# Transposing the maxima directly behind the value sums, and reading the memory in 64 by 64 quarters

## The chip, the cores and the metric

The kernel runs on one core of one Trainium2 chip. The metric is the device time of one launch in microseconds. In a profile the engines are called PE (TensorE's matmuls), PEld (its weight loads), DVE (VectorE), ACT (ScalarE), POOL (GpSimd) and SP (SyncE, which issues most transfers); ACTq and SPq are the queues of ScalarE and SyncE where they issue a transfer.

## The reference

Four attention layers, A B A B, each with a layer norm ahead and a residual add behind, over a sequence of 2048 tokens, width 512, 32 heads of 16. A is linear attention with a learned feature map. B, which the change touches, is causal-style softmax attention in four segments of 512 tokens with a compressive memory (the mask adds -1e9 to every later-indexed key):

```python
for s in range(N):                                   # N = 4 segments
    qs, ks, vs = q[:, :, s], k[:, :, s], v[:, :, s]
    logits = jnp.einsum("bhqd,bhkd->bhqk", qs, ks) * scale + mask
    p = _softmax(logits, axis=-1)
    a_dot = jnp.einsum("bhqk,bhkd->bhqd", p, vs)
    pq = phi(qs)
    num = jnp.einsum("bhld,bhde->bhle", pq, M)
    den = jnp.einsum("bhld,bhd->bhl", pq, z)[..., None] + 1e-6
    a_mem = num / den
    o = g * a_mem + (1.0 - g) * a_dot
    outs.append(o)
    pk = phi(ks)
    M = M + jnp.einsum("bhld,bhle->bhde", pk, vs)
    z = z + jnp.einsum("bhld->bhd", pk)
```

## The kernel before, in words

All engines' instruction orders are written out by hand: every instruction is tied to the one before it on its engine, so each engine works strictly in the order in which the program emits. Layer B is emitted by `steps`, a loop over slots. The work is cut into 32 half-blocks `m` per layer (4 segments, 4 groups of eight heads, 2 halves of four heads), and each half-block has five slots; slot `m.j` of a segment is its slot j of half-block m (0 to 7).

Each slot first emits one step of `attend` (logits into the PSUM tile `lg`, which has one buffer; then one exponential of 128 x 1024 on ScalarE into a `P` tile, and a triangular select on GpSimd) and one step of `maxima` (query-key products of a half-block two ahead, whose row maxima VectorE takes from PSUM with `mask` added; results in `mxs`). Then come functions put aside in the slot before (`self.later`), and jobs filed under the slot's number (`self.at`: copies and casts of projections, on ScalarE, VectorE and GpSimd). In a slot m.0 `weighted` follows: the value sums of the half-block just finished, 16 matmuls with 32 columns of the array each, into one `g` tile, which ScalarE copies, scaled by `share`, into `U`. After that the slot's own words from the tables FIRST (segment 0), GAPS (segments 1 and 2), LAST and FINAL (segment 3 of the first and the second layer B) are carried out from left to right:

- `max` is `put_maxima`: the 128 x 16 maxima are transposed on TensorE into a `g` tile, ScalarE copies them negated into `mt`, and ScalarE's own queue issues the transfer of `mt` into row 63 of the query stack `Q` that `attend` of the next half-block uses.
- `fin` is `finish`: four transposes of `U` into a `g` tile, then `weigh` on VectorE: a reciprocal and a multiplication, which read the `g` tile.
- `a0` to `a3` are `reads` of the memory for head groups 0 to 3 of this segment (`a0+`: of the next): `phi` of the queries (`tb` tiles) times `kn` (`mem`). Each word does one half: a `g` tile, two plain fp32 matmuls of the whole array, 136 wide, then `weigh` with three instructions on VectorE. `kn` holds zeros outside its own heads: rows 0 to 63 serve heads 0 to 3 of the group, rows 64 to 127 heads 4 to 7.
- `t`, `m` are the two steps of `writes` (four transposes of key features; then 16 small matmuls and the update of the memory on VectorE and GpSimd); `turn` is four transposes of finished outputs with a copy on ScalarE and a subtraction on VectorE (`oh`, `ol`); `ln` is a step of the next norm, in these places `columns`: four transposes with a copy and a subtraction (`hh`, `hl`).
- In slots m.1 to m.4 stand the large products in quarters: `Q` (query and key projection, two at once), `V` (values, two at once), `O` and `P` (output projections, two at once). Each such pair takes two `g` tiles when it begins and runs half the rows of the array for one and half for the other, in turns.

The PSUM tag `g` has four buffers of one bank each (`G = 4`); a tile takes the one that came free first, and its first matmul waits until the previous owner's last reader is done. Slots m.2 and m.4 use two `g` tiles for the maxima (`SPARE`), m.0, m.1 and m.3 the tiles `mx` and `my`. Helpers record every operation, so in the profile L178 is every matmul, L182 every transpose, and L156 nearly everything else.

Of the kernel before, what the change touches and what calls it, by code (L numbers as in the profile page):

```python
# [7 lines left out]
F32 = mybir.dt.float32  # L8
F32R = mybir.dt.float32r
BF16 = mybir.dt.bfloat16  # L10
AF = mybir.ActivationFunctionType
# [7 lines left out]
P = 128  # L19
# [3 lines left out]
VW = DH + 1  # L23
# [7 lines left out]
MT = 2  # L31
G = 4
# [20 lines left out]


FIRST = """
0.0 max            | 0.2 Q2/6          | 0.3 Q2/12         | 0.4 Q2/6
1.0 t0 fin max     | 1.1 Q3/6          | 1.2 Q3/6          | 1.3 Q3/6 | 1.4 Q3/6
2.0 m0 ln ln ln ln max fin | 2.1 V+/6     | 2.2 V+/6 w        | 2.3 V+/6 | 2.4 V+/6 w
3.0 t1 fin max     | 3.1 V+/6          | 3.2 V+/6 w        | 3.3 V+/6 | 3.4 V+/6 w
4.0 m1 max fin     | 4.1 Q0+/6 load    | 4.2 Q0+/6         | 4.3 Q0+/6 | 4.4 Q0+/6  # L60
5.0 t2 fin max     | 5.1 V+/6          | 5.2 V+/6 n        | 5.3 V+/6 n | 5.4 V+/6
6.0 m2 t3 fin max  | 6.1 Q1+/6         | 6.2 Q1+/6 n       | 6.3 Q1+/6 n | 6.4 Q1+/6
7.0 m3 a0+ a0+ max fin | 7.1 V+/6      | 7.2 V+/6 n        | 7.3 V+/6 n | 7.4 V+/6
"""
GAPS = """
0.0 a1 a1 max fin  | 0.1 Q2/6 n        | 0.2 Q2/6 n        | 0.3 Q2/6 n | 0.4 Q2/6
1.0 t0 turn fin max | 1.1 Q3/6      | 1.2 Q3/6 n        | 1.3 Q3/6 | 1.4 Q3/6
2.0 m0 turn t1 fin ln max | 2.1 O/6    | 2.2 O/6           | 2.3 O/6 | 2.4 O/6
3.0 m1 turn turn fin ln max | 3.1 O/6  | 3.2 O/6           | 3.3 O/6 | 3.4 O/6
4.0 ln ln a2 fin a2 max | 4.1 Q0+/6 load | 4.2 Q0+/6       | 4.3 Q0+/6 | 4.4 Q0+/6  # L70
5.0 t2 a3 fin max  | 5.1 V+/6 begin  | 5.2 V+/6 n N      | 5.3 V+/6 n N | 5.4 V+/6
6.0 m2 a3 t3 fin max | 6.1 Q1+/6       | 6.2 Q1+/6 n N     | 6.3 Q1+/6 n N | 6.4 Q1+/6
7.0 m3 a0+ a0+ max fin | 7.1 V+/6      | 7.2 V+/6 n N      | 7.3 V+/6 n N | 7.4 V+/6
"""
LAST = """
0.0 a1 a1 max fin  | 0.1 Q2/6 n        | 0.2 Q2/6 n        | 0.3 Q2/6 n | 0.4 Q2/6
1.0 turn max fin   | 1.1 Q3/6          | 1.2 Q3/6 n        | 1.3 Q3/6 | 1.4 Q3/6
2.0 turn ln fin max | 2.1 O/6          | 2.2 O/6           | 2.3 O/6 | 2.4 O/6
3.0 turn turn fin ln max | 3.1 O/6     | 3.2 O/6           | 3.3 O/6 | 3.4 O/6
4.0 ln ln a2 fin a2 max | 4.1 v/2      | 4.2 v/2           | 4.3 v/2 | 4.4 v/2  # L80
5.0 a3 a3 max fin  | 5.1 v/1           | 5.2 v/1           | 5.3 v/1 | 5.4 v/1
6.0 max fin        | 6.1 v/1           | 6.2 v/1           | 6.3 v/1 | 6.4 v/1 pre
7.0 pt pt fin max  | 7.1 P/4           | 7.2 P/5           | 7.3 P/5 v/2 | 7.4 P/4 v/2
"""
FINAL = """
0.0 a1 a1 max fin  | 0.1 Q2/6          | 0.2 Q2/6          | 0.3 Q2/6 | 0.4 Q2/6
1.0 turn turn max fin | 1.1 Q3/6       | 1.2 Q3/6          | 1.3 Q3/6 | 1.4 Q3/6
2.0 max fin        | 2.1 O/6           | 2.2 O/6           | 2.3 O/6 | 2.4 O/6
3.0 a2 a2 max fin  | 3.1 O/6           | 3.2 O/6           | 3.3 O/6 | 3.4 O/6
4.0 turn turn fin max | 4.1 O/6        | 4.2 O/6           | 4.3 O/6 | 4.4 O/6  # L90
5.0 a3 a3 max fin  | 5.1 O/6           | 5.2 O/6           | 5.3 O/6 | 5.4 O/6
6.0 max fin pre    | 6.1 pt pt         | 6.2 P/6           | 6.3 P/6 | 6.4 P/6
7.0 pt pt max fin  | 7.1 P/4           | 7.2 P/5           | 7.3 P/5 | 7.4 P/4
"""
BEFORE = {-25: "q0 load", -23: "v0", -21: "k0",
          -18: "n", -17: "v1 n", -16: "n", -15: "n n", -14: "q1 n", -13: "n", -12: "k1 n", -11: "n", -10: "v2 n",
# [4 lines left out]
def interleave_kernel(ctx, tc, x_in, a_wqkv, a_wphi, a_wo, b_wq, b_wk, b_wv, b_wo, b_beta,  # L101
# [15 lines left out]
    def nm(s):  # L117
        uid[0] += 1
        return f"{s}_{uid[0]}"

    def T2(tag, bufs, dt=F32, shape=(P, 512)):
        return sp.tile(list(shape), dt, tag=tag, bufs=bufs, name=nm(tag))

    def PS(tag, bufs, shape=(P, 512)):
        return ps.tile(list(shape), F32, tag=tag, bufs=bufs, name=nm(tag))
# [38 lines left out]
    dve, act, pool, sync = [Ordered(e) for e in (nc.vector, nc.scalar, nc.gpsimd, nc.sync)]  # L164

    def held(i):

        if last[0] is not None:
            behind(i, last[0])
        last[0] = i  # L170
        return i
# [3 lines left out]
    def mm(*a, **k):  # L175
        n = a[0].free_size()
        work[0] += n / 2.26 if k["rhs"].dtype == F32R else (n * 2 / 2.4 + 25 if "tile_position" in k else 2 * max(112, n * 2 / 2.4))
        return held(nc.tensor.matmul(*a, **k))  # L178

    def tp(*a):  # L180
        work[0] += 108
        return held(nc.tensor.transpose(*a))  # L182
# [338 lines left out]
    def weigh(out, p, eps, add, eng=pool):  # L521

        n, G = out.shape[1], out.shape[2]
        r = T2("r", 4, shape=(P, n, G))
        den = p[:, :, :, DH]
        if eps:
            dve.tensor_scalar(r, den, eps, None, op0=ADD)
            den = r
        dve.reciprocal(r, den)
        rb = r.unsqueeze(3).broadcast_to([P, n, G, DH])  # L530
        if not add:
            dve.tensor_tensor(out=out, in0=p[:, :, :, 0:DH], in1=rb, op=MUL)
            return
        t = T2("wt", 1, shape=(P, n, G, DH))
        dve.tensor_tensor(out=t, in0=p[:, :, :, 0:DH], in1=rb, op=MUL)
        eng.tensor_tensor(out=out, in0=out, in1=t, op=ADD)
# [441 lines left out]
    class LayerB:  # L978
# [97 lines left out]
        def reads(self, s, c):  # L1076

            kn = self.kn[:, c]
            ph = self.st[s, c]["phi", 0]
            ot = self.sums(s, c).rearrange("p q (h d) -> p q h d", d=DH)  # L1080
            for a in range(2):
                pn = PS("g", G)
                for q in range(2):
                    mm(pn[:, q * 8 * VW : (q + 1) * 8 * VW],
                       lhsT=ph[:, (2 * a + q) * P : (2 * a + q + 1) * P], rhs=kn,
                       start=True, stop=True)
                weigh(ot[:, 2 * a : 2 * a + 2], pn[:, 0 : 16 * VW].rearrange("p (q h e) -> p q h e", q=2, h=8),
                      1e-6, False)
                yield

        def writes(self, s, c):

# [76 lines left out]
        def put_maxima(self, m):  # L1169
            s, c, hf = m // 8, m % 8 // 2, m % 2  # L1170
            Q = self.st[s, c]["set"][0][:, 2 * hf : 2 * hf + 2, :]
            pt = PS("g", G)
            tp(pt[0:16, 0:P], self.mx.pop(m), ident)
            mt = T2("mt", MT, F32R, shape=(16, P))
            act.activation(mt, pt[0:16, 0:P], AF.Copy, scale=-1.0)
            act.dma_start(out=Q[63:P:64].bitcast(F32), in_=mt.bitcast(F32))

        def attend(self, m):

# [286 lines left out]
    for i in range(2):  # L1466
# [3 lines left out]
        a2 = la[i].pass2()  # L1470
# [40 lines left out]
```

## Time and profile before

| | us |
|---|---|
| median of 3 runs (lowest, highest) | 1433.65 (1431.13, 1434.63) |
| the profiled execution, its time | 1431.15 |
| the profiled execution, span from first to last instruction | 1429.4 |

The granted TensorE clock was 0.997 of full speed over the span. The two layers B lie at about 300 to 720 us and 1000 to 1420 us. In the rows a plain fp32 matmul or transpose of 128 x 128 or more counts as it was executed: one plain fp32 matmul of the program appears as two instructions, so the eight `g<-mem,tb` of a slot are four calls. A row of the timeline has the start in us, the duration, engine, line, operation, output<-inputs by tile names, shapes, and how many were merged; in square brackets stands idle time just before, and what ended it. Names may be of the tile that last held the memory (a `Q` stack is `e`).

### The profile page before, as it was taken

What the parts mean: (1) busy time and instruction counts of PE and PEld (TensorE: products, weight loads), DVE (VectorE), ACT (ScalarE), POOL (GpSimd) and SP (SyncE); (2) the same over time, 40 slices, a digit from 0 to 9 for tenths busy, and PEclk for the clock granted to TensorE, in tenths of its full rate; (3) what the DMA queues carried; (4) which work ended last, traced back from release to release, by engine and by line L of the source; (5) the groups of instructions that cost most, each with busy time, mean ns of one, the idle gap of its engine ahead of it and who ended that gap; (6) DMA issues with size and microseconds to landing.
All of it is one profiled execution on the core that took longest, in us unless ns stands there. A gap on an engine that the chain in (4) does not pass through costs nothing.

```text
span 1429.4 us, 34847 instructions
## 1 busy us (share of the span) xinstructions
PE 1357.6 (95%) x13120; PEld 1044.7 (73%) x13120; DVE 1054.6 (74%) x3259; ACT 809.2 (57%) x1198; POOL 688.3 (48%) x1052
## 2 busy tenths in 40 slices
PE   7999989999999999999899999999999999999997
PEld 6887878766667777777568887887766767767764
DVE  4666778577787887888646767867678878868882
ACT  5545345436667677676534433453566756756653
POOL 1568656414447447344314446542335556544441
PEclk9999999999999999999999999999999999999999
DMA  5397356535445454445430103854464554544431
GB/s 195 107 329 271 113 156 207 169 102 151 139 126 139 128 130 139 129 123 167 140 128 20 60 30 128 247 169 122 128 184 100 137 154 98 138 124 98 113 83 67
DMA packets 108792, 196.14 MB, mean 137 GB/s; under 512 B 14416, under 2 KB 27856, under 8 KB 107856
## 3 DMA queue, kind: packets, MB, share of 16 engines
q1 hardware_dynamic: 107472, 193.38, 46.1%
q8 instruction: 104, 1.70, 0.5%
q10 hardware_dynamic: 1152, 0.52, 0.1%
q14 instruction: 64, 0.52, 0.1%
HBM read 101.05 MB, written 39.85 MB: 99 GB/s over the span
## 4 chain that ended last, share of the span: by engine, by line
PE 65%; DVE 14%; ACT 7%; POOL 5%; DMA 4%; issue 3%; SPq 1%; ACTq 0%; DVEq 0%; POOLq 0%
PE g L178 49%; PE lg L178 6%; PE g L182 4%; ACT P L156 3%; PE mx L178 3%; DMA wqk<-wqk 2%; DVE es L156 2%; POOL tb L156 2%; POOL P L156 2%; PE my L178 1%; PE lg L182 1%; DVE g L156 1%; DVE my L156 1%; DVE mx L156 1%; SPq L156 1%
## 5 line engine op out<-in xcount | busy, mean ns | idle before, releaser
L156 ACT ACTIVATE P<-lg 128x1024 f32<-128x1024 f32 x320 | 329.3, 1029 | 183.3 <-PE lg L178 98.0
L156 POOL TENSOR_SCALAR_AFFINE_SELECT P<-P 128x256 f32<-128x256 f32 (+1 forms) x448 | 192.0, 443 | 338.2 <-ACT P L156 337.5
L178 PE MATMUL g<-hh,wqk 64*128 64x512 f32 (+1 forms) x960 | 193.3, 393 | 7.5 <-DMA wqk<-wqk 2.9
L156 DVE CUSTOM_DVE_ANT_0 mx<-mx,mask 128x128 f32<-128x128 f32 (+3 forms) x332 | 165.0, 497 | 37.7 <-PE my L178 31.5
L156 DVE CUSTOM_DVE_ANT_0 g<-g,mask 128x512 f32<-128x512 f32 x360 | 175.9, 544 | 15.7 <-PE g L178 15.1
L178 PE MATMUL g<-w,oh 64*128 64x512 f32 (+2 forms) x816 | 173.9, 388 | 6.8 <-SPq L156 5.0
L156 DVE CUSTOM_DVE_ANT_0 my<-my,mask 128x128 f32<-128x128 f32 (+3 forms) x332 | 172.1, 518 | 0.0
L178 PE MATMUL lg<-e,e 64*128 64x256 f32 (+2 forms) x1024 | 156.3, 353 | 15.1 <-ACT P L156 14.4
L178 PE MATMUL g<-P,v 128*32 128x512 f32 (+3 forms) x2048 | 151.1, 435 | 4.2 <-DVE mxs L156 4.0
L178 PE MATMUL g<-w,hh 64*128 64x512 f32 (+2 forms) x800 | 145.4, 357 | 1.0 <-DVE ol L156 0.6
L156 DVE DVE_READ_ACCUMULATOR2_ANT mxs<- 128x1 f32 x1024 | 143.8, 140 | 0.0
L178 PEld LDWEIGHTS lg<-e,e 64*128 64x128 f32 x1024 | 94.9, 185 | 62.9 <-ACT P L156 40.6
L178 PEld LDWEIGHTS g<-hh,wqk 64*128 64x128 f32 (+1 forms) x960 | 113.8, 185 | 24.5 <-issue 5.2
L178 PEld LDWEIGHTS g<-P,v 128*32 128x32 f32 x2048 | 59.7, 109 | 88.9 <-issue 65.6
L156 POOL TENSOR_SCALAR tb<-tb 128x512 f32<-128x512 f32 x72 | 110.8, 1551 | 25.4 <-ACT tb L156 25.4
L178 PEld LDWEIGHTS g<-w,oh 64*128 64x128 f32 (+1 forms) x816 | 99.7, 188 | 28.5 <-SPq L156 9.6
L178 PE MATMUL g<-hl,wqk 64*128 64x512 f32 (+1 forms) x480 | 113.4, 391 | 0.4 <-DVE hl L156 0.4
L178 PE MATMUL g<-w,ol 64*128 64x512 f32 (+2 forms) x408 | 108.4, 381 | 1.0 <-DVE ol L156 1.0
L178 PEld LDWEIGHTS g<-w,hh 64*128 64x128 f32 (+1 forms) x800 | 92.0, 187 | 13.8 <-DVE ol L156 1.0
L178 PE MATMUL g<-w,hl 64*128 64x512 f32 (+2 forms) x400 | 93.7, 355 | 0.0
L156 ACT COPY tb<-g 128x512 f32<-128x512 f32 (+1 forms) x124 | 66.8, 575 | 44.8 <-PE g L178 44.5
L178 PE MATMUL mx<-e,e 63*128 63x256 f32 (+2 forms) x332 | 89.5, 331 | 0.3 <-DVE mxs L156 0.3
(150 smaller groups left out, 2909.1 us busy)
## 6 DMA issues: line engine op xcount, KB each, us to landing
e<-ta SPq DMA_DIRECT2D x384, 128.0 KB
wqk<-wqk SPq DMA_DIRECT2D x64, 512.0 KB
x<-x SPq DMA_DIRECT2D x48, 256.0 KB
ot<-in SPq DMA_DIRECT2D x28, 256.0 KB
pq<-tb SPq DMA_DIRECT2D x24, 256.0 KB
tb<-pq SPq DMA_DIRECT2D x24, 256.0 KB
x<-xr SPq DMA_DIRECT2D x22, 256.0 KB
xr<-x SPq DMA_DIRECT2D x20, 256.0 KB
```

The costliest lines, as they stand in the source:

```text
L156: i = f(*a, **k)
L178: return held(nc.tensor.matmul(*a, **k))
L182: return held(nc.tensor.transpose(*a))
```

## The change

Two things. First, `put_maxima` is split: the transpose stays at the word `max`, and the copy into `mt` with its transfer is put aside and emitted in the next slot, behind that slot's steps of `attend` and `maxima`. With it the word `max` moves in every table to the front of its slot, behind `weighted` (and behind `m`, where there is one), and `fin` to the end (but for `pre`). Second, `reads` does a whole head group at one word: two `g` tiles, one for heads 0 to 3 and one for heads 4 to 7, filled by 16 matmuls of 64 rows by 64 columns, 68 wide; then two `weigh`. Words `a1 a1` become `a1`, and so on; those that stood apart are joined (`a3` of slots 5.0 and 6.0 in 5.0).

```diff
--- before.py
+++ after.py
@@ -53,44 +53,44 @@
 
 
 FIRST = """
-0.0 max            | 0.2 Q2/6          | 0.3 Q2/12         | 0.4 Q2/6
-1.0 t0 fin max     | 1.1 Q3/6          | 1.2 Q3/6          | 1.3 Q3/6 | 1.4 Q3/6
-2.0 m0 ln ln ln ln max fin | 2.1 V+/6     | 2.2 V+/6 w        | 2.3 V+/6 | 2.4 V+/6 w
-3.0 t1 fin max     | 3.1 V+/6          | 3.2 V+/6 w        | 3.3 V+/6 | 3.4 V+/6 w
-4.0 m1 max fin     | 4.1 Q0+/6 load    | 4.2 Q0+/6         | 4.3 Q0+/6 | 4.4 Q0+/6
-5.0 t2 fin max     | 5.1 V+/6          | 5.2 V+/6 n        | 5.3 V+/6 n | 5.4 V+/6
-6.0 m2 t3 fin max  | 6.1 Q1+/6         | 6.2 Q1+/6 n       | 6.3 Q1+/6 n | 6.4 Q1+/6
-7.0 m3 a0+ a0+ max fin | 7.1 V+/6      | 7.2 V+/6 n        | 7.3 V+/6 n | 7.4 V+/6
+0.0 max | 0.2 Q2/6          | 0.3 Q2/12         | 0.4 Q2/6
+1.0 max t0 fin | 1.1 Q3/6          | 1.2 Q3/6          | 1.3 Q3/6 | 1.4 Q3/6
+2.0 m0 max ln ln ln ln fin | 2.1 V+/6     | 2.2 V+/6 w        | 2.3 V+/6 | 2.4 V+/6 w
+3.0 max t1 fin | 3.1 V+/6          | 3.2 V+/6 w        | 3.3 V+/6 | 3.4 V+/6 w
+4.0 m1 max fin | 4.1 Q0+/6 load    | 4.2 Q0+/6         | 4.3 Q0+/6 | 4.4 Q0+/6
+5.0 max t2 fin | 5.1 V+/6          | 5.2 V+/6 n        | 5.3 V+/6 n | 5.4 V+/6
+6.0 m2 max t3 fin | 6.1 Q1+/6         | 6.2 Q1+/6 n       | 6.3 Q1+/6 n | 6.4 Q1+/6
+7.0 m3 max a0+ fin | 7.1 V+/6      | 7.2 V+/6 n        | 7.3 V+/6 n | 7.4 V+/6
 """
 GAPS = """
-0.0 a1 a1 max fin  | 0.1 Q2/6 n        | 0.2 Q2/6 n        | 0.3 Q2/6 n | 0.4 Q2/6
-1.0 t0 turn fin max | 1.1 Q3/6      | 1.2 Q3/6 n        | 1.3 Q3/6 | 1.4 Q3/6
-2.0 m0 turn t1 fin ln max | 2.1 O/6    | 2.2 O/6           | 2.3 O/6 | 2.4 O/6
-3.0 m1 turn turn fin ln max | 3.1 O/6  | 3.2 O/6           | 3.3 O/6 | 3.4 O/6
-4.0 ln ln a2 fin a2 max | 4.1 Q0+/6 load | 4.2 Q0+/6       | 4.3 Q0+/6 | 4.4 Q0+/6
-5.0 t2 a3 fin max  | 5.1 V+/6 begin  | 5.2 V+/6 n N      | 5.3 V+/6 n N | 5.4 V+/6
-6.0 m2 a3 t3 fin max | 6.1 Q1+/6       | 6.2 Q1+/6 n N     | 6.3 Q1+/6 n N | 6.4 Q1+/6
-7.0 m3 a0+ a0+ max fin | 7.1 V+/6      | 7.2 V+/6 n N      | 7.3 V+/6 n N | 7.4 V+/6
+0.0 max a1 fin | 0.1 Q2/6 n        | 0.2 Q2/6 n        | 0.3 Q2/6 n | 0.4 Q2/6
+1.0 max t0 turn fin | 1.1 Q3/6      | 1.2 Q3/6 n        | 1.3 Q3/6 | 1.4 Q3/6
+2.0 m0 max turn t1 fin ln | 2.1 O/6    | 2.2 O/6           | 2.3 O/6 | 2.4 O/6
+3.0 m1 max turn turn fin ln | 3.1 O/6  | 3.2 O/6           | 3.3 O/6 | 3.4 O/6
+4.0 max a2 ln ln fin | 4.1 Q0+/6 load | 4.2 Q0+/6       | 4.3 Q0+/6 | 4.4 Q0+/6
+5.0 max a3 t2 fin | 5.1 V+/6 begin  | 5.2 V+/6 n N      | 5.3 V+/6 n N | 5.4 V+/6
+6.0 m2 max t3 fin | 6.1 Q1+/6       | 6.2 Q1+/6 n N     | 6.3 Q1+/6 n N | 6.4 Q1+/6
+7.0 m3 max a0+ fin | 7.1 V+/6      | 7.2 V+/6 n N      | 7.3 V+/6 n N | 7.4 V+/6
 """
 LAST = """
-0.0 a1 a1 max fin  | 0.1 Q2/6 n        | 0.2 Q2/6 n        | 0.3 Q2/6 n | 0.4 Q2/6
-1.0 turn max fin   | 1.1 Q3/6          | 1.2 Q3/6 n        | 1.3 Q3/6 | 1.4 Q3/6
-2.0 turn ln fin max | 2.1 O/6          | 2.2 O/6           | 2.3 O/6 | 2.4 O/6
-3.0 turn turn fin ln max | 3.1 O/6     | 3.2 O/6           | 3.3 O/6 | 3.4 O/6
-4.0 ln ln a2 fin a2 max | 4.1 v/2      | 4.2 v/2           | 4.3 v/2 | 4.4 v/2
-5.0 a3 a3 max fin  | 5.1 v/1           | 5.2 v/1           | 5.3 v/1 | 5.4 v/1
-6.0 max fin        | 6.1 v/1           | 6.2 v/1           | 6.3 v/1 | 6.4 v/1 pre
-7.0 pt pt fin max  | 7.1 P/4           | 7.2 P/5           | 7.3 P/5 v/2 | 7.4 P/4 v/2
+0.0 max a1 fin | 0.1 Q2/6 n        | 0.2 Q2/6 n        | 0.3 Q2/6 n | 0.4 Q2/6
+1.0 max turn fin | 1.1 Q3/6          | 1.2 Q3/6 n        | 1.3 Q3/6 | 1.4 Q3/6
+2.0 max turn ln fin | 2.1 O/6          | 2.2 O/6           | 2.3 O/6 | 2.4 O/6
+3.0 max turn turn fin ln | 3.1 O/6     | 3.2 O/6           | 3.3 O/6 | 3.4 O/6
+4.0 max a2 ln ln fin | 4.1 v/2      | 4.2 v/2           | 4.3 v/2 | 4.4 v/2
+5.0 max a3 fin | 5.1 v/1           | 5.2 v/1           | 5.3 v/1 | 5.4 v/1
+6.0 max fin | 6.1 v/1           | 6.2 v/1           | 6.3 v/1 | 6.4 v/1 pre
+7.0 max pt pt fin | 7.1 P/4           | 7.2 P/5           | 7.3 P/5 v/2 | 7.4 P/4 v/2
 """
 FINAL = """
-0.0 a1 a1 max fin  | 0.1 Q2/6          | 0.2 Q2/6          | 0.3 Q2/6 | 0.4 Q2/6
-1.0 turn turn max fin | 1.1 Q3/6       | 1.2 Q3/6          | 1.3 Q3/6 | 1.4 Q3/6
-2.0 max fin        | 2.1 O/6           | 2.2 O/6           | 2.3 O/6 | 2.4 O/6
-3.0 a2 a2 max fin  | 3.1 O/6           | 3.2 O/6           | 3.3 O/6 | 3.4 O/6
-4.0 turn turn fin max | 4.1 O/6        | 4.2 O/6           | 4.3 O/6 | 4.4 O/6
-5.0 a3 a3 max fin  | 5.1 O/6           | 5.2 O/6           | 5.3 O/6 | 5.4 O/6
-6.0 max fin pre    | 6.1 pt pt         | 6.2 P/6           | 6.3 P/6 | 6.4 P/6
-7.0 pt pt max fin  | 7.1 P/4           | 7.2 P/5           | 7.3 P/5 | 7.4 P/4
+0.0 max a1 fin | 0.1 Q2/6          | 0.2 Q2/6          | 0.3 Q2/6 | 0.4 Q2/6
+1.0 max turn turn fin | 1.1 Q3/6       | 1.2 Q3/6          | 1.3 Q3/6 | 1.4 Q3/6
+2.0 max fin | 2.1 O/6           | 2.2 O/6           | 2.3 O/6 | 2.4 O/6
+3.0 max a2 fin | 3.1 O/6           | 3.2 O/6           | 3.3 O/6 | 3.4 O/6
+4.0 max turn turn fin | 4.1 O/6        | 4.2 O/6           | 4.3 O/6 | 4.4 O/6
+5.0 max a3 fin | 5.1 O/6           | 5.2 O/6           | 5.3 O/6 | 5.4 O/6
+6.0 max fin pre | 6.1 pt pt         | 6.2 P/6           | 6.3 P/6 | 6.4 P/6
+7.0 max pt pt fin | 7.1 P/4           | 7.2 P/5           | 7.3 P/5 | 7.4 P/4
 """
 BEFORE = {-25: "q0 load", -23: "v0", -21: "k0",
           -18: "n", -17: "v1 n", -16: "n", -15: "n n", -14: "q1 n", -13: "n", -12: "k1 n", -11: "n", -10: "v2 n",
@@ -1078,15 +1078,17 @@
             kn = self.kn[:, c]
             ph = self.st[s, c]["phi", 0]
             ot = self.sums(s, c).rearrange("p q (h d) -> p q h d", d=DH)
-            for a in range(2):
-                pn = PS("g", G)
-                for q in range(2):
-                    mm(pn[:, q * 8 * VW : (q + 1) * 8 * VW],
-                       lhsT=ph[:, (2 * a + q) * P : (2 * a + q + 1) * P], rhs=kn,
-                       start=True, stop=True)
-                weigh(ot[:, 2 * a : 2 * a + 2], pn[:, 0 : 16 * VW].rearrange("p (q h e) -> p q h e", q=2, h=8),
-                      1e-6, False)
-                yield
+            pns = [PS("g", G)[:, 0 : 16 * VW] for _ in range(2)]
+            for q in range(4):
+                for a, pn in enumerate(pns):
+                    for b in (0, 64):
+                        mm(pn[b : b + 64, q * 4 * VW : (q + 1) * 4 * VW],
+                           lhsT=ph[64 * a : 64 * a + 64, q * P + b : q * P + b + 64],
+                           rhs=kn[64 * a : 64 * a + 64, 4 * a * VW : (4 * a + 4) * VW], start=True, stop=True,
+                           tile_position=(64 * a, b))
+            for a, pn in enumerate(pns):
+                weigh(ot[:, :, 4 * a : 4 * a + 4], pn.rearrange("p (q h e) -> p q h e", q=4, h=4), 1e-6, False)
+            yield
 
         def writes(self, s, c):
 
@@ -1171,9 +1173,12 @@
             Q = self.st[s, c]["set"][0][:, 2 * hf : 2 * hf + 2, :]
             pt = PS("g", G)
             tp(pt[0:16, 0:P], self.mx.pop(m), ident)
-            mt = T2("mt", MT, F32R, shape=(16, P))
-            act.activation(mt, pt[0:16, 0:P], AF.Copy, scale=-1.0)
-            act.dma_start(out=Q[63:P:64].bitcast(F32), in_=mt.bitcast(F32))
+
+            def put():
+                mt = T2("mt", MT, F32R, shape=(16, P))
+                act.activation(mt, pt[0:16, 0:P], AF.Copy, scale=-1.0)
+                act.dma_start(out=Q[63:P:64].bitcast(F32), in_=mt.bitcast(F32))
+            self.later.append(put)
 
         def attend(self, m):
```

## The prediction

> **What bounds the kernel now.** I read the page first: the busy shares, then the chain that ended last.
>
> ```profile
> span 1429.4 us, 34847 instructions
> PE 1357.6 (95%) x13120; PEld 1044.7 (73%) x13120; DVE 1054.6 (74%) x3259; ACT 809.2 (57%) x1198; POOL 688.3 (48%) x1052
> PE 65%; DVE 14%; ACT 7%; POOL 5%; DMA 4%; issue 3%; SPq 1%; ACTq 0%; DVEq 0%; POOLq 0%
> ```
>
> TensorE is busy nearly throughout, so in the attention loop a microsecond taken from it should be a microsecond saved, unless something else comes late in its place. The edit touches only the first slot of each group of five (m.0) and the start of the next (m.1), so I read the timeline there. This is slot 0.0 of a later segment, in order of time (start, duration, engine, operation):
>
> ```profile
> 618.47 2.36 PE L178 MATMUL g<-P,v 128*32 128x512 f32 x32
> ...
> 619.87 0.13 DVE L156 DVE_READ_ACCUMULATOR2_ANT mxs<- 128x1 f32 x1
> ...
> 620.76 1.19 PE L178 MATMUL g<-mem,tb 128*128 128x136 f32 x8
> 620.89 0.69 ACT L156 ACTIVATE U<-g,share 128x512 f32<-128x512 f32 x1 [0.79 <-PE g L178]
> 621.53 0.17 DVE L156 TENSOR_SCALAR r<-g 128x16 f32<-128x16 f32 x1 [0.98 <-PE g L178]
> ...
> 621.79 0.27 PE L182 MATMUL g<-ident,mxs 128*16 128x128 f32 x1
> ...
> 621.90 0.60 PE L182 MATMUL g<-ident,U 128*128 128x128 f32 x4
> 622.02 0.42 DVE L156 TENSOR_TENSOR ot<-g,r 128x256 f32<-128x256 f32 x1
> 622.10 0.27 ACT L156 ACTIVATE mt<-g 16x128 fp32r<-16x128 f32 x1 [0.53 <-PE g L182]
> 622.37 0.16 DVE L156 TENSOR_SCALAR r<-g 128x16 f32<-128x16 f32 x1
> ...
> 622.43 0.50 PE L178 MATMUL lg<-e,e 64*128 64x512 f32 x2
> ...
> 623.04 1.03 ACT L156 ACTIVATE P<-lg 128x1024 f32<-128x1024 f32 x1 [0.67 <-PE lg L178]
> 623.07 0.40 PE L178 MATMUL g<-hh,wqk 64*128 64x512 f32 x2
> ```
>
> From the start of the value sums (618.47 = 0): sums until 2.29, memory's reads until 3.32, the transpose of the maxima (T) 0.11, the transposes of `finish` 0.53, then slot 0.1 with logits and maxima 0.64, and at 4.60 the projection pair begins. TensorE waits nowhere. Every item in it but the logits and maxima takes one of the four `g` banks of PSUM, and the pair takes two at once. That pool is the thing to watch. It does stall TensorE already where a slot uses many banks, as in slot 3.0:
>
> ```profile
> 450.20 0.60 PE L182 MATMUL g<-ident,U 128*128 128x128 f32 x4
> 450.64 0.60 PE L182 MATMUL g<-ident,x 128*128 128x128 f32 x4
> 451.33 0.28 PE L182 MATMUL g<-ident,mxs 128*16 128x128 f32 x1
> ...
> 450.59 1.29 DVE L156 TENSOR_TENSOR ol<-g,oh 128x512 fp32r<-128x512 f32 x2 [0.99 <-ACT oh L156]
> ```
>
> Four transposes take 0.44 (450.20 to 450.64), so T should stand at 451.08. It comes at 451.33, when the first of VectorE's two `ol` subtractions (about half of the 1.29) has read its bank. T's input, the maxima, was there two microseconds before.
>
> **The reads.** Now 8 instructions take 1.03 (620.76 to 621.79). Afterwards there are 16 calls, 32 instructions, of 64 rows by 64 columns and 68 wide. No such quadrant with plain fp32 is in the trace. The nearest rows are the reads of the other layer, 68 wide in two column halves:
>
> ```profile
> 185.94 1.17 PE L178 MATMUL g<-KN,P 128*64 128x68 f32 x32 [1.15 <-ACT P L156]
> 187.04 1.09 PE L182 MATMUL lg<-ident,P 128*128 128x128 f32 x8
> ...
> 185.94 1.05 PE L178 MATMUL g<-KN,P 128*64 128x68 f32 x28 [1.15 <-ACT P L156]
> ```
>
> The last four of 32 add 0.12, so a pair of tiles side by side takes 0.06. Sixteen pairs make 0.96, and 1.10 passed: 0.14 goes into entering and leaving this shape of the array. Four quadrants abreast would give 8 x 0.06 + 0.14 = 0.62, a saving of 0.41; only two abreast, 1.10, a loss of 0.07. I take 0.62, because the value sums in 32-column strips do run abreast (618.47: 32 instructions in 2.29, 0.07 each for widths of 128 to 512, where the present reads, 136 wide, take 0.13 each), and keep 1.10 for the range.
>
> A rule of the Trainium skill speaks against this part: TensorEngine Tiling (Array Packing), under Key Properties, says that a change of tiling mode drains TensorE. T and `finish` use the whole array, so each read now pays two changes where it had none behind T. The 0.14 above agrees with the rule; without it the sum below would be at most 24 x 0.14 = 3.4 lower.
>
> **Slot 0.0 after the change, step by step.** T at 2.29 (the maxima are there at 619.87 + 0.13, that is 1.53); reads 2.40 to 3.02. `finish` cannot start before ScalarE has copied the sums, 620.89 + 0.69 = 3.11 and some 0.06 of signal: 3.17. So 0.15 of the 0.41 is gone here. Then 0.53 + 0.64: TensorE is ready for the pair at 4.34.
>
> Its banks are not. The four are: the sums' (taken over by `finish`), T's, and two for the reads. T's is now read in slot 0.1 behind the softmax's exponential. That one starts 0.61 after the logits (622.43 to 623.04), here 3.70 + 0.61, and takes 1.03; `mt` takes 0.27: free at 5.5. VectorE reaches the reads 0.77 after they begin (620.76 to 621.53). Then four instructions filled one bank in about half a microsecond; now both banks fill together in the same time, so again 0.77: 3.17. One division occupies VectorE 0.84 (621.53 to 622.37) and frees its bank after 0.91 (622.02 + 0.42). First bank 4.08, second 3.17 + 0.84 + 0.91 = 4.92. The pair's second matmul starts at about 4.97, against 4.60 now: **+0.37**, although TensorE has less to do. Today the pair gets T's bank (copied by 622.37) in place of the second read's.
>
> The same page of the Trainium skill (Performance Considerations, PSUM Bottleneck) says that tiling speeds up TensorE and not the emptying of PSUM. The row agrees: 0.84 a bank stays while the reads shrink. Without that limit the first rival below would hold.
>
> **The other opening slots.** The same steps, with these rows (7.0; 4.0; 5.0; the last of each is the next big matmul in slot m.1):
>
> ```profile
> 605.89 2.36 PE L178 MATMUL g<-P,v 128*32 128x512 f32 x32
> 608.26 0.14 DVE L156 DVE_READ_ACCUMULATOR2_ANT mxs<- 128x1 f32 x1
> 608.61 0.19 DVE L156 TENSOR_TENSOR mem<-g,mem 128x34 f32<-128x34 f32 x1 [0.20 <-PE g L178]
> 610.78 0.63 PE L178 MATMUL g<-w,hh 64*128 64x512 f32 x4
> ...
> 461.42 2.36 PE L178 MATMUL g<-P,v 128*32 128x512 f32 x32
> 467.23 0.54 PE L178 MATMUL g<-hh,wqk 64*128 64x512 f32 x2
> ...
> 475.11 2.36 PE L178 MATMUL g<-P,v 128*32 128x512 f32 x32
> 479.64 0.63 PE L178 MATMUL g<-w,hh 64*128 64x512 f32 x4
> ```
>
> - 7.0 (`m3 max a0+ fin`): T waits for the maxima, 608.40 = 2.51, so 2.67. The second read bank is the memory update's, free at 2.91; VectorE reaches the reads at 3.70, the second bank is free at 5.45, the pair at 5.5 against 4.89: +0.6, four times. In segment 0 the next slots wait on ScalarE anyway: +0.35, twice.
> - 4.0 (`max a2 ln ln fin`): reads to 3.02, first columns in the sums' bank at 3.17, second in the first read bank at 4.14, `finish` in the second at 4.98, then 0.5 + 0.64 and a short wait: 6.2 against 5.81: +0.4, five times with the last segment's.
> - 5.0 and 6.0: 5.0 now holds a whole read; `t2` at 3.17, `finish` at 4.14, the pair at 5.28 against 4.53: +0.75. 6.0 loses its half read (0.57) and a visible T (0.1): net +0.1, four times.
> - 0.0 and its like (`max a fin` before a pair): +0.37, eight times.
> - Slots with output turns and columns (2.0, 3.0, 4.0 of the last layer): one of four banks is held through the whole slot, so a later transpose waits for VectorE as T does in 3.0 above, some 0.4 longer in all; against this the exponential of m.1 no longer stands behind `mt`. I take +0.27, eleven times.
> - 1.0: costs nothing, since the pair of slot 1.1 waits for its weights. Its second matmul stands 1.25 behind the first, and 5.5 behind the load that was issued at the end of the pair before:
>
> ```profile
> 419.88 1.02 SPq L156 DMA_DIRECT2D wqk<-wqk  x2
> ...
> 424.14 0.46 PE L178 MATMUL g<-hh,wqk 64*128 64x512 f32 x1
> 425.39 0.47 PE L178 MATMUL g<-hh,wqk 64*128 64x512 f32 x1 [0.79 <-ACT P L156]
> ```
>
> - Segment 0, where the moved copy helps. `mt` and its DMA issue stand ahead of the exponential, which the next logits wait for:
>
> ```profile
> 349.39 0.50 PE L178 MATMUL lg<-e,e 64*128 64x512 f32 x2
> ...
> 349.79 0.51 ACTq L156 DMA_DIRECT2D e<-mt  x1
> 350.40 1.02 ACT L156 ACTIVATE P<-lg 128x1024 f32<-128x1024 f32 x1 [0.64 <-PE my L178]
> ...
> 351.48 0.56 PE L178 MATMUL lg<-e,e 64*128 64x256 f32 x4 [0.56 <-ACT P L156]
> ```
>
> The exponential could start at 349.39 + 0.61 = 350.00, 0.40 sooner. Behind it `mt` and the issue (0.27 + 0.52) then delay ScalarE's next cast, if there is one. 3.0: -0.3, twice; 5.0 and 6.0: -0.15, four times; 2.0, with four columns in three banks and a cast behind: +0.5, twice. Together -0.2. The DMA itself has three slots in hand instead of four, more than the 5.5 that two far larger loads took above.
>
> **Sum:** 4 x 0.6 + 2 x 0.35 + 5 x 0.4 + 4 x 0.1 + 8 x 0.37 + 11 x 0.27 - 0.2 = +11.2. The profiled execution took 1431.15 (span 1429.4), so 1442.4; the median of the three runs lies 2.5 higher, at 1433.65. I put the forecast between the two, 1443.5.
>
> **Rivals.**
> 1. Faster: the banks come free in time, and TensorE's saving counts. It needs the second read's bank some 0.6 sooner, at 4.34 in slot 0.0, by a quicker division or a copy of T ahead of the exponential. For it speaks the 95% of TensorE; against it the 0.84 a bank. Then 24 x 0.41 = 9.8, and about 2 for T under the wait for U: 1419.5.
> 2. Much slower: the row halves are not side by side. Reads cost 1.10, and each division, and so each bank, comes 0.48 later: 22 places without the hidden ones, +10.6 on top of the sum: 1453. The trace shows no fp32 row halves either way.
> 3. No change that can be measured: TensorE stands idle for parts of the loop already (0.56 at 351.48, 0.79 at 425.39), and such waits shrink when it arrives later. If they take up most of the 11: 1431 to 1437. Measurement of this kernel can tell about 0.3% (4.3 us).
>
> **How the numbers follow.** Forecast 0.52 (its own range 1438 to 1451), rival 1 0.20, rival 2 0.15, rival 3 0.13. So faster 0.20, same 0.13, slower 0.67. The range takes in rivals 2 and 3 and the upper edge of rival 1, where only some slots get their banks in time: 1428 to 1457.
>
> **What would show it.** Right: 32 reads in about 0.62 from first to next; T directly behind the sums; `mt` behind the first exponential; and in m.1 a gap of about 0.6 on TensorE within the pair's first two matmuls, released by VectorE's `ot` (or ScalarE's `mt`), with the pair some 5.0 behind the start of the sums in 0.0 and 5.5 in 7.0. Wrong: pairs that start at 4.4 with no gap (rival 1); reads of 1.1 (rival 2); or the gaps there, while idle time before logits and sums falls by as much (rival 3).

## The result, and the profile after

The changed kernel took 1445.78 us (median of six runs, 1443.42 to 1446.46) where the kernel before took 1433.83 in the same series (six runs, 1431.13 to 1436.21): a ratio of 1.0083, 95% interval 1.0068 to 1.0099. It is 12 us slower; forecast were 1443.5 in all, and +11.2 by the sum. The profiled execution took 1445.68.

The page of the kernel after, the lines that answer to those of before (span, busy time of each engine, chain that ended last):

```profile
span 1444.0 us, 35957 instructions
...
PE 1358.0 (94%) x13696; PEld 1055.3 (73%) x13696; DVE 1055.9 (73%) x3259; ACT 807.9 (56%) x1198; POOL 689.4 (48%) x1052
...
PE 68%; DVE 12%; ACT 7%; POOL 5%; issue 4%; DMA 3%; SPq 1%; ACTq 1%; DVEq 0%; POOLq 0%
```

TensorE has 576 instructions more and the same busy time; the span is 14.6 longer, so the loss is waiting. The equal busy time hides that the rows of the reads fell from 30.2 us to 18.7: what they saved came back elsewhere, in part because a matmul of a pair now runs alone while the other waits (below, x1 at 629.64, where the kernel before has x2 at 623.07). Here is slot 0.0 of the last segment again, in the timeline (start, duration, engine, line, operation):

```profile
625.25 2.36 PE L178 MATMUL g<-P,v 128*32 128x512 f32 x32
...
627.54 0.28 PE L182 MATMUL g<-ident,mxs 128*16 128x128 f32 x1
627.68 0.69 ACT L156 ACTIVATE U<-g,share 128x512 f32<-128x512 f32 x1 [0.89 <-PE g L178]
...
627.75 0.70 PE L178 MATMUL g<-mem,tb 64*64 64x68 f32 x32
...
628.42 0.66 PE L182 MATMUL g<-ident,U 128*128 128x128 f32 x4
628.49 0.17 DVE L156 TENSOR_SCALAR r<-g 128x16 f32<-128x16 f32 x1 [1.28 <-PE g L178]
...
629.32 0.17 DVE L156 TENSOR_SCALAR r<-g 128x16 f32<-128x16 f32 x1
...
629.64 0.40 PE L178 MATMUL g<-hh,wqk 64*128 64x512 f32 x1
629.81 0.42 DVE L156 TENSOR_TENSOR ot<-g,r 128x256 f32<-128x256 f32 x1
...
630.34 0.46 PE L178 MATMUL g<-hh,wqk 64*128 64x512 f32 x1 [0.29 <-issue]
...
630.53 0.25 ACT L156 ACTIVATE mt<-g 16x128 fp32r<-16x128 f32 x1
```

The 32 reads take 0.67 (627.75 to 628.42) in place of 1.03. The pair's first matmul comes 4.39 behind the start of the sums, 0.2 sooner than before. The second stands still until 5.09: VectorE's second division ends at 629.81 + 0.42 = 630.23, and the matmul follows 0.11 later. T's bank, the other one that could have served, is read only at 630.53. The tag at the second matmul says "issue", not VectorE; the order of the rows is what names the bank.

The waits of TensorE, grouped by what ended them (total us, times, longest), in the kernel before and then in the kernel after:

```profile
PE lg L178 <- ACT P L156: 14.4, 56, 0.6
...
PE g L178 <- SPq L156: 6.1, 6, 2.2
...
PE g L178 <- DVE mxs L156: 4.0, 9, 0.8
```

```profile
PE lg L178 <- ACT P L156: 15.4, 48, 0.8
...
PE g L178 <- DVE mxs L156: 5.8, 9, 1.1
...
PE g L182 <- DVE r L156: 4.3, 9, 0.5
...
PE g L178 <- DVE ot L156: 2.1, 6, 0.4
...
PE g L178 <- issue: 1.8, 6, 0.3
...
PE g L178 <- DVE tmp L156: 1.3, 3, 0.5
...
PE g L182 <- ACT KN L156: 1.0, 4, 0.2
```

The last five lines are new. Apart from "issue", they are transposes and pairs of products that wait for a `g` bank which the division (`r`, `ot`, `tmp`) or a copy gives back.

### The profile page after: what moved, and what is told of

The parts are those of the page before. It is cut to its first block, busy times and chain, and to the rows that moved or that the text cites. A ratio compares the mean times of both kernels' runs of the same rounds, so it can differ in the third digit from the quotient of the medians.

```text
span 1444.0 us, 35957 instructions
## 1 busy us (share of the span) xinstructions
PE 1358.0 (94%) x13696; PEld 1055.3 (73%) x13696; DVE 1055.9 (73%) x3259; ACT 807.9 (56%) x1198; POOL 689.4 (48%) x1052
## 4 chain that ended last, share of the span: by engine, by line
PE 68%; DVE 12%; ACT 7%; POOL 5%; issue 4%; DMA 3%; SPq 1%; ACTq 1%; DVEq 0%; POOLq 0%
PE g L178 51%; PE lg L178 6%; PE g L182 5%; ACT P L156 3%; PE mx L178 3%; POOL tb L156 2%; POOL P L156 2%; DVE es L156 2%; DMA wqk<-wqk 2%; PE my L178 2%; PE lg L182 1%; DVE r L156 1%; DVE tmp L156 1%; SPq L156 1%; DVE g L156 1%
## 5 line engine op out<-in xcount | busy, mean ns | idle before, releaser
L178 PE MATMUL g<-hh,wqk 64*128 64x512 f32 (+1 forms) x960 | 207.6, 396 | 10.0 <-DMA wqk<-wqk 3.7
L178 PE MATMUL lg<-e,e 64*128 64x256 f32 (+2 forms) x1024 | 165.8, 349 | 15.6 <-ACT P L156 15.4
L178 PE MATMUL g<-w,hh 64*128 64x512 f32 (+2 forms) x800 | 152.8, 359 | 4.2 <-DVE ot L156 2.1
L178 PEld LDWEIGHTS g<-hh,wqk 64*128 64x128 f32 (+1 forms) x960 | 131.8, 186 | 23.7 <-DVE r L156 3.8
L178 PEld LDWEIGHTS lg<-e,e 64*128 64x128 f32 x1024 | 107.4, 185 | 50.9 <-ACT P L156 32.8
L178 PE MATMUL g<-hl,wqk 64*128 64x512 f32 (+1 forms) x480 | 126.3, 395 | 0.4 <-DVE hl L156 0.4
L178 PEld LDWEIGHTS g<-w,oh 64*128 64x128 f32 (+1 forms) x816 | 102.7, 187 | 28.1 <-SPq L156 7.8
L178 PEld LDWEIGHTS g<-w,hh 64*128 64x128 f32 (+1 forms) x800 | 98.3, 186 | 18.0 <-PE my L178 4.5
L178 PE MATMUL g<-w,hl 64*128 64x512 f32 (+2 forms) x400 | 100.3, 355 | 0.0
```

## The experiments

Five kernels separate the three parts of the change (order of the words, copy put off, quarters) and its two suspects (T's bank, the second read bank). Then come the cast behind the late copy, the price of the quarters, and a version that keeps what helped. "Pair" is the start of the second large product behind the start of the value sums, in 0.0, 7.0, 4.0 and 5.0 of a later segment; "groups" are the times from one start of value sums to the next.

| kernel | order | copy | reads | median us | ratio to before (95%) | pair 0.0, 7.0, 4.0, 5.0 |
|---|---|---|---|---|---|---|
| before | old | at once | halves | 1433.8 | 1 | 4.60, 4.89, 5.88, 4.54 |
| after | new | late | quarters | 1445.8 | 1.0083 (1.0068 to 1.0099) | 5.09, 5.71, 6.33, 5.50 |
| a1 | new | at once | quarters | 1427.0 | 0.9949 (0.9927 to 0.9972) | 4.39, 5.02, 5.64, 4.82 |
| b1 | old | at once | quarters | 1428.3 | 0.9965 (0.9951 to 0.9980) | 4.40, 4.50, 5.89, 4.85 |
| c1 | new | late | halves | 1445.8 | 1.0083 (1.0060 to 1.0106) | 4.92, 5.33, 6.17, 5.35 |
| e1 | new | at once | halves | 1428.4 | 0.9978 (0.9966 to 0.9990) | 4.50, 4.90, 5.47, 4.95 |
| d1 | new | late | quarters, one division | 1430.5 | 0.9975 (0.9961 to 0.9989) | 4.41, 5.01, 5.82, 4.82 |

The kernel before had 1432.8 in the series of a1 to d1 and 1431.3 in that of e1, f1 and g1, so the ratios are compared, not the medians.

### The copy at once

```diff
-            self.later.append(put)
+            put()
```

> The changed kernel with one line undone: `mt` and its transfer are emitted at the word `max` again, not a slot later; order and quarters stay. Bank theory (T's bank, held until the copy behind the first exponential, makes the pair wait): T's bank is free at about 3.5 after the value sums begin, so the pair of slot 0.0 starts its second matmul at 4.4 and not 5.09 (eight such slots, -5.5), 7.0 at about 5.0 and not 5.70 (-2.8), 4.0 and 5.0 gain about 0.5 each (-4.5): 1430 to 1434. Division theory (both read banks come late because VectorE's two divisions start together; T's bank hardly matters): 0.0 stays above 4.9, 1442 to 1446. Quarter theory (the changes of array shape and the new order on TensorE cost the time): 1442 to 1446 as well, with the pair no earlier.

0.9949: that one line turns 12 us lost into 7 gained. The timeline of slot 0.0 of a1:

```profile
616.96 2.36 PE L178 MATMUL g<-P,v 128*32 128x512 f32 x32 [0.30 <-DVE mxs L156]
...
619.97 0.25 ACT L156 ACTIVATE mt<-g 16x128 fp32r<-16x128 f32 x1
...
621.34 0.40 PE L178 MATMUL g<-hh,wqk 64*128 64x512 f32 x2
...
621.53 0.42 DVE L156 TENSOR_TENSOR ot<-g,r 128x256 f32<-128x256 f32 x1
```

The copy ends at 620.22, 3.26 behind the start of the sums, and both matmuls of the pair start by 621.34 (4.39), while VectorE's second division is still to end (621.53 + 0.42). So the pair uses T's bank, as the bank theory says; the time came out 3 us below its range. The groups of 2.0 and 3.0 of segments 1 and 2 shrank too, by 0.3 and by 0.5 to 0.7 below the kernel before (one of 3.0 by 3.4), which no theory had counted; one group of 2.0, in the last segment of the first layer, grew by 2.9, with a wait of 1.5 for a subtraction (`ol`) of VectorE in it. Neither was followed to its cause.

### The quarters alone

The kernel before with `reads` of the change, and each pair of words joined at one place (`a1 a1 max fin` becomes `a1 max fin`, `ln ln a2 fin a2 max` becomes `ln ln a2 fin max`, `a3` of 5.0 and 6.0 stands in 5.0).

> The kernel before with its reads in quarters alone (the two words of a group joined at the place of the first; `max`, `fin` and the copy of the maxima as before). Bank theory: T's bank is copied within half a microsecond again, the pair of 0.0 starts at about 4.35 against 4.60, 7.0 at 4.5 against 4.89, slots 5.0 and 6.0 together gain 0.3 each: about -5, so 1427 to 1431. Division theory: the saving is lost wherever the second read bank is needed, 1432 to 1437. Quarter theory: most of the 12 us is here, 1440 or more.

0.9965, in the range of the bank theory: the pairs of 0.0 and 7.0 start 0.2 and 0.39 sooner. The gain that it gave 5.0 and 6.0 did not come: the groups of 5.0 went from 12.67, 12.66, 12.72, 12.41 to 13.61, 13.62, 13.62, 12.85, those of 6.0 lost only 0.36 to 0.38 each, so 1.7 more in all. A whole read in 5.0 costs more than the half read that 6.0 gets rid of. Nor do the groups show that the 5 us come from the bank: the eight of 0.0 and its like shrank by 2.0 in all, those of 7.0 by only 0.2 although the pair is 0.39 sooner, and most of the rest lies in slots that wait for loads (one group of 3.0 shorter by 2.9, one of 4.0 by 0.9, those of 1.0 by 1.3 in all). Where the gain of the medians lies stays open.

### The order and the late copy, with the old reads

```diff
         def reads(self, s, c):
...
-            pns = [PS("g", G)[:, 0 : 16 * VW] for _ in range(2)]
...
+            for a in range(2):
+                pn = PS("g", G)
+                for q in range(2):
+                    mm(pn[:, q * 8 * VW : (q + 1) * 8 * VW],
+                       lhsT=ph[:, (2 * a + q) * P : (2 * a + q + 1) * P], rhs=kn,
+                       start=True, stop=True)
+                weigh(ot[:, 2 * a : 2 * a + 2], pn[:, 0 : 16 * VW].rearrange("p (q h e) -> p q h e", q=2, h=8),
+                      1e-6, False)
+            yield
```

> The changed kernel with the reads in their old shape (two banks one after the other, whole-array matmuls, both halves at one word); the tables and the put-off copy stay. Bank theory: the pair waits for T's bank all the same, 0.0 at about 4.95, 5.0 at 5.4: 1441 to 1446. Quarter theory: without the quarters the loss goes, 1431 to 1436. Division theory: the first bank is divided half a microsecond sooner, about a third of the loss goes: 1439 to 1442.

1.0083, the same as with the quarters. The quarter theory falls: without one quarter in the program the whole loss is there. The old reads even start the pair sooner (4.92 against 5.09): in c1 they follow T in 0.12, where the quarters take 0.21 (627.54 to 627.75 above), and VectorE starts on their first bank 0.66 behind the first read, not 0.74. With the copy put off, the 0.36 that TensorE saves on each read buys nothing.

### One division left out

The second division of each read is replaced by a memset of its output, so nobody reads the second bank.

```diff
-            for a, pn in enumerate(pns):
-                weigh(ot[:, :, 4 * a : 4 * a + 4], pn.rearrange("p (q h e) -> p q h e", q=4, h=4), 1e-6, False)
+            weigh(ot[:, :, 0:4], pns[0].rearrange("p (q h e) -> p q h e", q=4, h=4), 1e-6, False)
+            dve.memset(ot[:, :, 4:8], 0.0)
```

> The changed kernel without the second division of each read: heads 4 to 7 of a group get zeros from a memset in place of their memory part, and the second read bank has no reader. Bank theory and division theory both say that the pair of 0.0 then takes that bank and starts at 4.4 (5.09 in the changed kernel), 7.0 at 5.0, 4.0 about 0.8 and 5.0 about 1.0 earlier: 1427 to 1432; it says what the held bank is worth when it is given back without moving the copy. Quarter theory: VectorE and banks are not what is late, 1441 to 1446.

0.9975, with the copy as late as in the change. Slot 0.0 of d1 in the timeline:

```profile
621.24 2.36 PE L178 MATMUL g<-P,v 128*32 128x512 f32 x32
...
624.98 0.43 DVE L156 TENSOR_TENSOR ot<-g,r 128x256 f32<-128x256 f32 x1
...
625.65 0.40 PE L178 MATMUL g<-hh,wqk 64*128 64x512 f32 x2
```

Both matmuls start at 4.41. For this pair one bank given back in time is enough, and it does not matter which: T's (a1) or the second read's (d1). 4.0 and 5.0 gained 0.5 and 0.7, less than the 0.8 and 1.0 expected; d1 also spares VectorE some 0.6 a read (a memset of 0.27 for a division of 0.83), so a part of its time may be that.

### The order alone, with the copy at once and the old reads

c1 with `put()` at the word `max`.

> The fourth corner: order of the changed kernel, old shape of the reads, and `mt` with its transfer emitted at the word `max`. Against c1_order_alone (1445.8) it differs by the copy alone, against a1_copy_at_once (1427.0) by the quarters alone, against the kernel before mostly by the order. Bank theory: the copy is worth as much here as with the quarters (19 us there), somewhat less because the old reads free their first bank sooner: 1428 to 1432, so the quarters are worth 1 to 4 us once no bank is late, and nothing with the late copy. If the quarters carried the gain of a1_copy_at_once, this one stays at 1436 or more; if the order costs something by itself, it comes out slower than the kernel before.

0.9978: slightly faster than before. Against c1 (1.0083) the late copy alone costs 1.0%, some 15 us; against a1 (0.9949) the quarters are worth 0.3%, 4 us, but the two intervals just overlap, and the medians of the two series differ by 1.4. The order by itself costs nothing in sum. So the late copy costs 15 us with the old reads and 19 with the quarters, and by the ratios the quarters gain some 4 to 5 with the copy at once and nothing behind a late one. A late copy in the old order was not built.

By the groups of the change less those of a1, 7 of the 19 us lie in the slots 0.0 and its like and 7.0, where the timelines show the bank. Slot 5.0 has 5.2, of which a cast accounts for the larger part (next section). The 5.0 in slots 2.0 and 3.0 and the 1.2 in 4.0 were not followed to their cause.

### What the late copy does besides

The forecast was most wrong in 5.0 (below). The timeline of the kernel after in slot 5.2, and at the start of 6.0:

```profile
482.87 0.25 ACT L156 ACTIVATE mt<-g 16x128 fp32r<-16x128 f32 x1
...
483.14 0.52 ACTq L156 DMA_DIRECT2D e<-mt  x1
...
483.66 0.14 DVE L156 DVE_READ_ACCUMULATOR2_ANT mxs<- 128x1 f32 x1
483.75 0.62 ACT L156 CAST ta<-tb 128x512 fp32r<-128x512 f32 x1 [0.64 <-ACT mt L156]
...
484.41 0.69 DVE L156 TENSOR_TENSOR ta<-tb,ta 128x512 fp32r<-128x512 f32 x1 [0.60 <-ACT ta L156]
...
490.56 1.02 PE L178 MATMUL g<-P,v 128*32 128x512 f32 x5 [0.64 <-DVE mxs L156]
```

The transfer's issue stands ahead of a cast on ScalarE, VectorE waits 0.60 for the cast, and six microseconds later the value sums of 6.0 wait 0.64 for VectorE's maxima. In f1 SyncE issues the transfer; nothing else differs.

```diff
-                act.dma_start(out=Q[63:P:64].bitcast(F32), in_=mt.bitcast(F32))
+                sync.dma_start(out=Q[63:P:64].bitcast(F32), in_=mt.bitcast(F32))
```

> The changed kernel with the put-off transfer of `mt` issued by SyncE in place of ScalarE; the copy stays late. In slot 5.2 of the changed kernel ScalarE issues that transfer (0.52) ahead of a cast, and VectorE, which needs the cast, stands idle 0.61 and is behind until the next value sums, which wait for its maxima. Cast theory: without the issue VectorE's idle time goes, the groups of slot 5.0 shrink by 0.5 to 1.0 (six), and 2.0 of segment 0 by 0.3 (two), with the pairs of slots x.1 where they are: 1440 to 1443. Bank theory alone: the banks come back at the same time, so no change, 1444 to 1447. If SyncE, which takes its transfers in order, is held by the wait for `mt`, its loads come later: 1447 or more.

```profile
481.96 0.25 ACT L156 ACTIVATE mt<-g 16x128 fp32r<-16x128 f32 x1
...
482.11 0.60 ACT L156 CAST ta<-tb 128x512 fp32r<-128x512 f32 x1
...
482.75 0.68 DVE L156 TENSOR_TENSOR ta<-tb,ta 128x512 fp32r<-128x512 f32 x1
```

VectorE's idle time is gone, and the groups of 5.0 shrink, from 14.09, 14.80, 14.07, 13.67 to 13.45, 14.42, 13.45, 13.19, and in segment 0 from 12.97, 12.98 to 12.23, 12.23: 3.6 us over the six. The pairs of 0.0, 7.0, 4.0 and 5.0 stand where they stood, to 0.01 (5.09, 5.70, 6.33, 5.50). The program as a whole did not get measurably faster: 1443.8, 1.0092 (1.0072 to 1.0112). Four groups of 3.0 grew by 0.3 to 0.5, and TensorE's waits on SyncE's queue went up:

```profile
PE g L178 <- SPq L156: 4.4, 5, 1.1
```

```profile
PE g L178 <- SPq L156: 8.6, 7, 2.2
```

(kernel after, then f1). So the cast is shown to be a part of what stretched 5.0. Where the gain went is shown only in part. The four waits in 3.0 went from 0.73 to 0.87 up to 1.17 to 1.20 each, 1.5 in all. The longest, 2.2, is new in slot 6.0 of the last segment of the first layer (its group grew by 2.0); the kernel before and c1 have one wait of 2.2 each on this queue too, each at another place, so whether this one comes of the change is open.

### The price of the quarters

Two kernels of which one execution each was taken (1460.7 and 1442.6 us, the kernel before 1428.1 beside them): every read emitted twice over (`for q in (0, 1, 2, 3, 0, 1, 2, 3)`), and the loops over `a` and `q` exchanged, so that all of rows 0 to 63 go ahead of rows 64 to 127.

> The changed kernel with every read emitted twice over (32 calls, 64 instructions, the second sixteen writing the same values again), to price the quarters apart from the entry and exit of their shape. If four quadrants run abreast and the rest of the 0.67 is a fixed price for the change of shape: 32 instructions more add 8 x 0.059 = 0.47, 1.14 from the first read to the next transpose or value product. If the quadrants are only two abreast and the 0.67 hides a late end: 0.9 more, about 1.6.

```profile
633.82 1.18 PE L178 MATMUL g<-mem,tb 64*64 64x68 f32 x64
...
634.93 0.55 PE L182 MATMUL g<-ident,U 128*128 128x128 f32 x3
...
635.03 0.17 DVE L156 TENSOR_SCALAR r<-g 128x16 f32<-128x16 f32 x1 [1.78 <-PE g L178]
```

Twice the reads take 1.11 (633.82 to 634.93), 0.44 more than 0.67, or 0.055 for four quadrants. The remaining 0.23 of a read does not grow with the number of matmuls; the prediction took 0.14 for it, as the change of shape. Here VectorE starts 1.21 behind the first read, 0.47 later than in the change.

> The changed kernel with the reads' loops exchanged: all of rows 0 to 63 (first bank), then all of rows 64 to 127 (second bank), the same sixteen calls. If row halves run abreast only when their calls alternate: 16 x 0.06 + 0.2, about 1.15 from the first read to what follows. If order makes no difference: 0.67. The division of the first bank can start about as early as now or 0.1 sooner, the second is ready only 0.5 later: the second matmul of the pair in 0.0 stays within 0.2 of 5.09 if VectorE's two divisions in a row set it.

```profile
628.59 0.99 PE L178 MATMUL g<-mem,tb 64*64 64x68 f32 x32
...
629.33 0.17 DVE L156 TENSOR_SCALAR r<-g 128x16 f32<-128x16 f32 x1 [1.27 <-PE g L178]
...
629.51 0.66 PE L182 MATMUL g<-ident,U 128*128 128x128 f32 x4
```

Row halves one after the other take 0.92 (628.59 to 629.51), neither of the two values: they do run abreast only when they alternate, and 0.25 is lost otherwise. Yet the pair of 0.0 stands at 5.09, to the hundredth where the changed kernel has it. VectorE starts its first division 0.74 behind the first read in both, because here the first bank is filled alone. In 7.0 the pair even comes sooner, at 5.49 (5.71). So a quarter of a microsecond more on TensorE in every read does not delay the pair; what counts is when the first bank is full and that two divisions follow.

### A version that is faster than both

g1 is b1 (quarters, copy at the word `max`) with `max` at the front only where a1 had the shorter groups:

(the first cells of the lines changed, several to a line)

```diff
 FIRST
-3.0 t1 fin max     | 5.0 t2 fin max     | 6.0 m2 t3 fin max
+3.0 max t1 fin     | 5.0 max t2 fin     | 6.0 m2 max t3 fin
 GAPS
-2.0 m0 turn t1 fin ln max | 3.0 m1 turn turn fin ln max | 5.0 t2 a3 fin max | 6.0 m2 t3 fin max
+2.0 m0 max turn t1 fin ln | 3.0 m1 max turn turn fin ln | 5.0 max a3 t2 fin | 6.0 m2 max t3 fin
```

> Quarters as in b1_quarters_alone with the copy at the word `max`, and `max` moved to the front only where a1_copy_at_once had the shorter groups: slots 3.0, 5.0 and 6.0 of segment 0 and 2.0, 3.0, 5.0 and 6.0 of segments 1 and 2. By the groups of those two runs: 2 x (0.52 + 0.39 + 0.29) + 4 x (0.32 + 0.6 + 0.5) = 8 us below b1_quarters_alone (1428.3) if each slot keeps what it had there: 1419 to 1423. If the slots are not independent (VectorE's backlog or SyncE's loads carry over from one to the next): 1424 to 1428.

1418.2 (1417.7 to 1419.4), 0.9911 (0.9895 to 0.9927): 13 us faster than before and, by the ratios, some 25 faster than the change. The slots kept what they had in a1 and b1: groups of 11.26 in 3.0 of segment 0 (before 11.77), 13.17 in 2.0 (13.49), 12.06 in 0.0 (12.27) and 12.54 in 7.0 (12.58). The slots 5.0 still lose (13.23 for 12.67). The gain in segment 0 is the one that the prediction saw for 3.0: with the copy in front, no copy and issue stand ahead of the exponential.

## Why the prediction was right, and where its terms were off

Forecast 1443.5, measured 1445.8; the mechanism was the one described, and each alternative has its run.

- **The banks.** Right. Slot 0.0: second matmul forecast at 4.97, measured 5.09. VectorE reached the reads 0.07 later than the sum had it (3.24 against 3.17), because the quarters followed T in 0.21 and not 0.11, and the matmul followed the division by 0.11, not 0.05. The cause is shown by a1 and d1 together: give back either bank and the pair starts at 4.4.
- **Rival 1** (banks in time). It did not happen in the change, but its condition was named rightly, a copy of T ahead of the exponential. a1 is that kernel and gained 7 us; 1419.5 was too much for it, and g1, with other places for `max`, got there.
- **Rival 2** (row halves not abreast). Ruled out: 0.67, not 1.10. By i1 even not alternating gives 0.92, and its premise, that slower reads delay the divisions, fails where the first bank is filled first.
- **Rival 3** (absorbed by idle time). The waits of logits for the exponential, where it was looked for, were 14.4 and are 15.4: nothing was absorbed there.
- **The reads.** 0.62 forecast, 0.67 measured: 0.44 for the products where 0.48 was taken, and 0.23 that does not grow with them (h1) where 0.14 was taken for the change of shape. That the 0.23 is the change of shape is inferred; no run has these reads without it. The Trainium skill's rule (TensorEngine Tiling (Array Packing), Key Properties), that a change of mode drains TensorE, agrees with the 0.23. It was not what made the kernel slower: c1 has no such reads and is as slow.

The sum, term by term, against the groups of the two profiled executions (time from one start of value sums to the next, after less before):

| term | forecast | measured |
|---|---|---|
| 0.0 and its like, eight | +3.0 | +3.6 |
| 7.0, six | +3.1 | +4.5 |
| 5.0 and 6.0 of the later segments, four of each | +0.4 | +3.5 |
| 4.0, five | +2.0 | +0.7 |
| turns and columns, eleven | +3.0 | -1.5 |
| 1.0 | 0 | +2.2 |
| segment 0 but 7.0 and 1.0 | -0.2 | +0.3 |
| slots not costed | 0 | +1.3 |
| together | +11.2 | +14.5 |

**5.0 and 6.0** is the term that was mis-sized most. 6.0 went as forecast (-0.66 to -0.68 for -0.67), so all of it is 5.0: +1.25 to +2.13 a group where +0.75 was taken. The pair stood at 5.50 for 5.28 forecast; `finish` waited for the first division's bank, as the sum had it, but until 4.30 and not 4.14. The larger part is VectorE: one division more, and the idle 0.60 behind the late copy's transfer; this is what made the value sums of 6.0 wait. The group of +2.13 also holds a wait of 1.1 on SyncE's queue; a1, b1 and g1 have one in the same place too (0.6 to 1.2), the kernel before, c1, d1 and e1 have none; why is open. The prediction had seen that the copy and its issue delay "ScalarE's next cast, if there is one", but priced it in segment 0 only. f1 shows the cast: 0.4 to 0.75 a group. It also takes back +0.69 in 2.0 of the last segment of the second layer, a slot that was not costed at all (11.48, 12.17, and 11.47 in f1). b1, which has no late copy, still loses 0.9 in three of the four groups of 5.0, and that is the whole read.

**7.0** is the same bank as 0.0, a little later than thought. The timeline of 7.0, kernel after:

```profile
611.80 2.36 PE L178 MATMUL g<-P,v 128*32 128x512 f32 x32
...
614.66 0.99 PE L178 MATMUL g<-mem,tb 64*64 64x68 f32 x32
...
616.94 0.42 DVE L156 TENSOR_TENSOR ot<-g,r 128x256 f32<-128x256 f32 x1
...
617.51 0.70 PE L178 MATMUL g<-w,hh 64*128 64x512 f32 x3 [0.30 <-DVE ot L156]
```

The reads took 0.92 here (614.66 to `finish` at 615.58), as their second bank was still the memory update's. VectorE came to them at 3.81 (forecast 3.70), the second bank was free at 5.56 (5.45), and the pair came at 5.71, not 5.5.

**Turn slots** were taken at +0.27. Those of 2.0 measured +0.11 to +0.13; three of the four of 3.0 measured +0.13, +0.13 and +0.21, the fourth -2.53, where the longest wait on SyncE's queue of the execution before (2.2, quoted above) is missing after. In 1.0 one group grew by 2.91, with waits of 1.2 for the load of `wqk` and of 0.8 for VectorE's maxima in it, and one of 4.0 shrank by 0.51, with a wait of 0.7 on SyncE's queue gone. These three nearly cancel (-0.1). Without them the turn slots are +1.1, and 4.0 has three groups of +0.41 to +0.43, as forecast, and one of -0.11. Whether such waits for loads move by the change or by chance was not tried. (In the rows of 3.0 on which the term rests, T's maxima had been there for 2.9 us before T could start, not two; nothing hangs on it.) That the sum of 11.2 came so near the medians' 12.0 is therefore partly luck: turns too dear, 5.0 and 7.0 too cheap. Within 0.0 and its like, too, two misses offset each other: the six of 0.0 measured +0.42 to +0.58, the two of the last layer +0.15 and +0.17, for +0.37.

## What to carry to other kernels

When a shared pool of PSUM banks feeds the next large product, cost an edit by when the banks come back, not by the engine time that it saves: the same 0.36 per read was worth, by the ratios, some 4 to 5 us with one bank free and nothing without. Here a small copy that empties a bank belonged ahead of the long operation on its engine, although its result is needed much later; that one line decided between 12 us lost and 7 gained. And of a step that is moved, follow every instruction to the next user of its new place: the transfer's issue of 0.52 reached TensorE through a cast and VectorE, six microseconds later.

## What the runs showed of the hardware that was not expected

- Four 64 by 64 quadrants of plain fp32, 68 wide, run abreast at 0.055 per four (h1: 0.44 for 32 more), row halves into different banks included, but only if the matmuls alternate between the row halves: 0.67 a read, against 0.92 with one half behind the other (i1).
- A read in that shape has a part of 0.23 that does not grow with the number of matmuls (0.67 less the 0.44 that sixteen more take), more than the 0.14 that the two column halves of the other layer had suggested. Ahead of it the quarters follow T 0.09 later than whole-array reads do (0.21, in c1 0.12).
- A transfer issued by ScalarE occupies it for 0.52, and a cast behind it starts 0.64 later than the engine's last work. Issued by SyncE instead, it left the cast alone (f1), but the four waits on SyncE's queue in 3.0 grew by 0.3 to 0.5 each.
